# Attention followed by a feed-forward layer: two products split by head pair, two casts on ScalarE

## The chip, the cores and the metric

The kernel runs on one core of one Trainium2 chip. Five engines work side by side and meet at semaphores: TensorE (PE in the profile; its weight loads are shown as PEld), VectorE (DVE), ScalarE (ACT), GpSimd (POOL) and SyncE (SP), which here only issues DMAs. The metric is device time in microseconds; of several runs the median is taken. Lower is better.

## The reference

```python
# q, k, v: [8 batches, 8 heads, 576 positions, 64], float32
scores = (1 / 8) * q @ k^T                       # per batch and head
mask   = (i // 64) >= (j // 64)                  # causal in blocks of 64
attn   = softmax(where(mask, scores, -1e9))
x      = (attn @ v), heads side by side          # 4608 rows x 512
h      = x @ w_in                                # 512 -> 2048
g      = h * sigmoid(beta * h)
out    = g @ w_out                               # 2048 -> 512, float32
```

## The kernel before

**Attention.** Work is cut into 32 units `u = 4 * b + c`: a batch `b` and a pair of heads `c`. For the first two batches (`b < QB`) each unit's Q and K come by DMA into a float32 staging tile `ST` (L618, on SP's queue; six slots), are cast to bf16 into `QKn` (L625; POOL does most, DVE those named by `onp`), transposed on PE (L634) and copied from PSUM to `QKT` by DVE (L642). From batch 2 on the transposition is a DMA (L672). Scores are matmuls of `QKT` on 64-row tiles (L708, and L443 where a loaded weight is used again). ACT takes the exponential into `E` (L724, L736), DVE zeroes masked corners (L730, L732), PE multiplies with `V` (L764), DVE takes reciprocals of the sums (L776) and normalises into `xq` (L783; ACT does it for unit 1 in ten small copies, L788). For the first three batches PE transposes `xq` (L813) and DVE or, for units 2 and 3, ACT copies it to `xT` (L823, L821); later a DMA does it (L800). `xT` holds the feed-forward input with features on the partitions: slice `c` of it comes from head pair `c`.

**Feed-forward.** Nine chunks `r` of 512 rows. For each of 16 column blocks `j` of `w_in`, PE adds four 128-feature matmuls in one PSUM bank (L1000, function `fh`, one matmul for each head pair `c`), ACT takes a tanh (L1010), DVE forms `gT` (L1014). The second product is written plainly for chunk 0 (L1036) and as a seven-product scheme on half tiles for the others (L921).

**Order.** Nothing in the code fixes the engines' instruction order by hand. Every operation is entered with `P.op(engine, duration, function, deps, tiles, prio)`; `Plan.schedule` walks through a modelled time and gives each free engine the ready operation of lowest `prio` (on PE ties go to the earlier entered, elsewhere to the earlier ready). It hands out buffer slots and PSUM banks as it goes; an operation that gets a slot waits for the last users of it. So a small change of durations or priorities can reorder everything planned after it, and the waits with it. PE also gets filler matmuls (L523, L525) in modelled time before 50 us. `pr(u)` gives the attention priorities: 40 to 70 for batch 1; the feed-forward operations of chunk 0 have 1000 + `j`.

What the change touches: the cast of Q and K (`fn`, L625), the priority of the copy to `QKT` (`fc`, L642) and the creation of the first product (`fh`, L1000), whose dependencies `xd` name the `xT` copies of all four pairs of the batches in the chunk. Chunk 0 lies inside batch 0, so `xd` has four entries there.

Of the kernel before, what the change touches and what calls it, by code (L numbers as in the profile page):

```python
# [4 lines left out]
ACT = mybir.ActivationFunctionType  # L5
# [354 lines left out]
def bass_blockwise_causal_attn__then__act_swish_beta_kernel(  # L360
# [10 lines left out]
    with es:  # L371
        def sb(name, shape, dt):
# [5 lines left out]
        PARTS = [((0, 4, "SP", range(6)), (4, 8, "SP", range(2)), (4, 8, "POOL", range(2, 6)))] + [((0, 8, "SP", range(6)),)] * 7  # L378
        GROUPS = [((0,), (1,), (2,), (3,))] + [((0, 1), (2, 3))] * 7
        NS = 6  # L380
        JOIN = (2,3,4,5,6,7)
        NO = 4
        FAST = range(1, NRC)
# [4 lines left out]
        ST6 = [s[0:96].rearrange("p t d -> p (t d)")[:, 768 * i:768 * i + 768].rearrange("p (h j d) -> p h j d", h=2, j=6)  # L388
               for s in ST for i in range(3)]
# [4 lines left out]
        QKn = [sb(f"QKn{i}", [128, 2, 2, 768], bf16) for i in range(NQ)]  # L394
# [26 lines left out]
        P = Plan()  # L421
# [6 lines left out]
        def mm(n):  # L428
            return max(n / 2.4 + 3, 55.0)
# [4 lines left out]
        def dve_t(n):  # L434
            return (n + 125) / 0.96
# [34 lines left out]
        for i in range(NQ):  # L470
# [5 lines left out]
            o = P.op("POOL", 200, mk(lambda g, i=i: g.memset(Vn[i][:, 4, :, 64:66], 0.0)), prio=-5)  # L476
# [6 lines left out]
        for i in range(NQ, NE + 1):  # L483
# [8 lines left out]
                  deps=[bt, c2], tiles=[tb], lat=400, mode="full", prio=5)  # L492
# [5 lines left out]
        win, wout = [], []  # L498
# [18 lines left out]
        for i in range(NFILL):  # L517
# [10 lines left out]
            n = 125  # L528
            o = P.op("PE", n, ff, deps=[c2, c4], tiles=[tf], lat=n, mode="full", prio=1e6 + i)
# [6 lines left out]
        for b in range(B):  # L536
            ts, t = P.tile("Vs"), P.tile("V")
# [3 lines left out]
            for h0, h1, e, tt in PARTS[b]:  # L541

                vs = []
                for i in tt:
# [9 lines left out]
                    n = (h1 - h0) / 8 * (1 if i < 4 else 0.25)  # L554
                    if e == "SP":
                        o = P.op("SP", 300 + 550 * n, fv, tiles=[ts], xfer=1400 * n,
                                 prio=3.5 + 0.1 * (h0 > 0) if b == 0 else 4 * b + (3.5 if b < 2 else 0.5),
                                 dma=["d_V", h0, 1])
                    else:
                        o = P.op("POOL", 150 + 1450 * n, fv, tiles=[t], xfer=1400 * n, prio=-30 if b == 0 else 4 * b + (3.5 if b < 2 else 0.5), dma=["d_VP", h0, 1])  # L560
# [8 lines left out]
                n = 5 if 4 in tt else len(tt)  # L569
                for g0 in range(h0, h1, 2):  # L570
                    g1 = g0 + 2

                    def fw(g, e, ts=ts, t=t, g0=g0, g1=g1, n=n):
                        return g.tensor_copy(Vn[t.slot][:, 0:n, g0:g1, 0:64], Vs[ts.slot][:, 0:n, g0:g1, :])  # L574

                    o = P.op("POOL", 60 + 60 * n * (g1 - g0), fw, deps=[*vs, *ones, *vzero], tiles=[ts, t],
                             prio=4 * b + 0.5 - (38.5 - 4.6 * (h0 > 0)) * (b < 1))
# [23 lines left out]
        for u in range(NU):  # L601
            b, c = divmod(u, NPAIR)
            Tv = tl[b]
            p = c % 2
            if p == 0:

                tn, tt_ = P.tile("QKn"), P.tile("QKT")
                turned = []
                casts = []
            if b < QB:  # L610

                turned = []
                for w, (nm, src) in enumerate((("Q", q), ("K", k))):
                    ts, pt = P.tile("ST"), P.tile("P1")
                    early6.append(ts)

                    def fl(g, e, ts=ts, src=src, b=b, c=c):
                        return [g.dma_start(ST6[ts.slot].rearrange("p h j d -> p h (j d)"),  # L618
                                            src[b, 2 * c:2 * c + 2].rearrange("h (p j) d -> p h (j d)", j=6))]

                    o = ld[nm, u] = P.op("SP", 420, fl, tiles=[ts], xfer=1170, prio=u, dma=["d_S", 0, 1])
                    o.pkt = 80.0

                    def fn(g, e, ts=ts, tn=tn, p=p, w=w):
                        return g.tensor_copy(QKn[tn.slot][0:96, p, w, :].rearrange("p (j h d) -> p j h d", j=6, h=2),  # L625
                                             ST6[ts.slot].rearrange("p h j d -> p j h d"))

                    onp = u not in (0, 3) or w == 1
                    o = P.op("POOL" if onp else "DVE", 850 if onp else 750, fn, deps=[o], tiles=[ts, tn],
                             prio=-40 + 3 * u if onp else -1)  # L630

                    def ft(g, e, tn=tn, pt=pt, p=p, w=w):
                        for i in range(6):
                            z = g.transpose(PSb[:, pt.slot, 96 * i:96 * i + 96],  # L634
                                            QKn[tn.slot][0:96, p, w, 128 * i:128 * i + 128], identB[0:96, 0:96])
                        return z

                    o = P.op("PE", 6 * 43, ft, deps=[o, c4], tiles=[tn, pt, tt_], lat=6 * 43 + 170, mode="full",
                             prio=pr(u))

                    def fc(g, e, pt=pt, td=tt_, p=p, w=w):
                        return g.tensor_copy(QKT[td.slot][:, p, w, 0:576].rearrange("c (p j) -> c p j", j=6),  # L642
                                             PSb[:, pt.slot, 0:576].rearrange("c (j p) -> c p j", j=6))

                    o.rest = 400.0 if b else 0.0

                    turned.append(P.op("DVE", dve_t(576), fc, deps=[o], tiles=[pt, tt_], prio=-5 if b < 1 else .5))
            elif p == 0:

                for w, (nm, src) in enumerate((("Q", q), ("K", k))):  # L650
                    ts = P.tile("S4")

                    def fl(g, e, ts=ts, src=src, b=b, c=c):
                        return [g.dma_start(STh[ts.slot], src[b, 2 * c:2 * c + 4].rearrange("h t d -> (h t) d").rearrange(
                            "(i p) d -> p i d", p=128))]

                    o = P.op("SP", QKI, fl, deps=[o for t in early6 for o in t.users] if b == QB else [],
                             tiles=[ts], xfer=QKX, prio=u, dma=["d_S4", 0, 1])
                    for i in range(2):
                        ld[nm, u + i] = o  # L660
                    for a in range(2):
                        def fn(g, e, ts=ts, tn=tn, a=a, w=w):
                            x = STh[ts.slot][:, 9 * a:9 * a + 5, :]
                            x = bass.AP(x.tensor, x.offset, [x.ap[0], [64, 5], [256, 2], [1, 64]])
                            return g.tensor_copy(  # L665
                                QKn[tn.slot][:].rearrange("p a w n -> p (a w n)")[:, 640 * (2 * a + w):][:, 0:640]
                                .rearrange("p (t h d) -> p t h d", t=5, h=2), x)

                        casts.append(P.op(CAST, 740, fn, deps=[o], tiles=[ts, tn], prio=u))

                def ft(g, e, tn=tn, td=tt_):
                    return [g.dma_start_transpose(QKT[td.slot][:].rearrange("c a w (t n) -> c (a w t) n", n=128),  # L672
                                                  QKn[tn.slot][:].rearrange("p a w n -> p (a w n)")[:, 0:2560])]

                turned = [P.op("SP", 3250, ft, deps=casts, tiles=[tt_, tn], xfer=3200, prio=-1, dma=["d_T", 0, 1])]
# [3 lines left out]
            if b not in JOIN or p == 0:  # L679
# [4 lines left out]
                for grp in visits:  # L684
# [3 lines left out]
                    def fq(g, e, pst=pst, grp=grp, tqk=tqk, b=b):  # L688
                        keep = {}
                        for (uu, g0), ps in zip(grp, pst):  # L690
# [4 lines left out]
                            for t, q0, q1, off in blocks:  # L695
# [17 lines left out]
                    n = sum(220 if g0 < 3 else 60 for _, g0 in grp)  # L713
                    o = P.op("PE", n, fq, deps=cps, tiles=list({id(x): x for x in pst}.values()) + [tqk] + [tes[uu] for uu in sorted({uu for uu, _ in grp})] * (b > 0),
                             lat=n + 200, mode="row", prio=pr(u) + .2 if len(grp) == 4 else pr(u + 1) + .1 if grp[0][0] > u else
# [4 lines left out]
            for g0 in range(4):  # L720
                o, ps = qk[g0]
# [76 lines left out]
            if b >= XB:  # L798
# [5 lines left out]
                n = len(blocks(b))  # L804
# [184 lines left out]
        for r in range(NRC):  # L989
            row = RC * r  # L990
# [4 lines left out]
            for j in range(NJ):  # L995
                ph, tt = P.tile("P1"), P.tile("th")

                def fh(g, e, ph=ph, j=j, row=row):
                    for c in range(4):
                        z = g.matmul(PS[:, ph.slot, :], w_in[:, c, 128 * j:128 * j + 128], xT[:, c, row % RX:row % RX + RC],  # L1000
                                     start=(c == 0), stop=(c == 3))
                    return z

                o = P.op("PE", 4 * mm(512), fh, deps=xd + [win[j // 4]], tiles=[ph, tg], lat=4 * mm(512) + 170,
                         mode="full", prio=1000 + 100 * r + j)

                hs.append(o)

                def fs(g, e, ph=ph, tt=tt, j=j):
                    return g.activation(th[tt.slot][:], PS[:, ph.slot, :], ACT.Tanh, scale=beta[:, j:j + 1])  # L1010
                a = P.op("ACT", act_t(512, 1), fs, deps=[o, bC], tiles=[ph, tt], lat=act_t(512, 1) + 93, prio=0)

                def fg(g, e, ph=ph, tt=tt, tg=tg, j=j):
                    return g.scalar_tensor_tensor(out=gT[tg.slot][:, j, :], in0=th[tt.slot][:], scalar=1.0,  # L1014
                                                  in1=PS[:, ph.slot, :], op0=ALU.add, op1=ALU.mult)
                gs.append(P.op("DVE", dve_t(512), fg, deps=[a] + (spare.users + spare_x.users if r == 1 else []), tiles=[ph, tt, tg], prio=0))
# [113 lines left out]
```

## Time and profile before

| | us |
|---|---|
| median of 5 runs | 334.65 |
| lowest and highest | 334.15, 339.23 |
| the profiled execution, its own time | 335.34 |
| its span, first to last instruction | 333.5 |
| busy: PE | 322.7 (97%) |
| busy: DVE, ACT, POOL | 222.5, 213.0, 85.5 |
| mean granted clock of TensorE | 0.995 |

The span begins with the first instruction and is 1.84 us shorter than the execution's own time. Busy shares are means over stages with different limits; matmul durations are modelled at their ends, so a busy PE can still be slower than its best. In the rows for DMAs, SPq is SP's queue: the time beside a row is how long the issuing took, not how long the transfer did. The groups that the change touches, each with its count, busy time, mean in ns and idle time of the engine before it:

```profile
L1000 PE MATMUL PS<-xT,w_in 128*128 128x512 bf16 x542 | 130.7, 381 | 2.8 <-issue 0.5
```

### The profile page before, as it was taken

The page shows a single profiled execution, that of the slowest core. Times are in us where ns is not written, and L with a number is a line of the kernel's source. Part 1 is how long each engine was busy: PE and PEld are TensorE (multiplying, and loading weights), DVE is VectorE, ACT ScalarE, POOL GpSimd, SP SyncE. Part 2 cuts the span into 40 slices and gives each one's busy share as a digit, 9 for nine tenths or more (in the row PEclk, how much of TensorE's full clock was granted, in tenths as well). Part 3 has the DMA queues.
Part 4 walks back from the last instruction along what each step waited for, and adds up shares of the span by engine and source line. Part 5 has one row for each costly group of instructions (what it writes and reads, how often), then busy time and mean ns, then how long its engine had stood idle before and what let it go on. Part 6 is the DMA issues. An engine that isn't in the chain of part 4 may idle for free.

```text
span 333.5 us, 7478 instructions
## 1 busy us (share of the span) xinstructions
PE 322.7 (97%) x3112; PEld 204.5 (61%) x3090; DVE 222.5 (67%) x448; ACT 213.0 (64%) x324; POOL 85.5 (26%) x127
## 2 busy tenths in 40 slices
PE   7988999999999999999999999999999999999996
PEld 4565445544677457764676567566466766666685
DVE  4637866479783697457966595668567685666742
ACT  2865994189357886768758857884885645544521
POOL 7746182074082053103520630330000000000000
PEclk9997999999999999999999999999999999999999
DMA  7999999999999999999999998977102210110023
GB/s 199 225 234 234 200 217 210 195 279 221 204 268 216 159 206 195 211 206 198 194 191 198 203 269 185 192 134 132 34 31 41 85 51 33 44 52 31 0 97 126
DMA packets 154993, 53.41 MB, mean 160 GB/s; under 512 B 139072, under 2 KB 154448, under 8 KB 154960
## 3 DMA queue, kind: packets, MB, share of 16 engines
q1 hardware_dynamic: 141200, 40.19, 62.2%
q0 software_dynamic: 5568, 4.36, 8.3%
q10 hardware_dynamic: 8192, 8.39, 8.1%
q8 instruction: 24, 0.39, 0.5%
q14 instruction: 9, 0.07, 0.1%
HBM read 36.71 MB, written 9.44 MB: 138 GB/s over the span
## 4 chain that ended last, share of the span: by engine, by line
PE 83%; DVE 4%; ACT 4%; DMA 2%; issue 2%; SPq 2%; POOL 1%; ACTq 0%; POOLq 0%
PE PS L1000 34%; PE PS L921 28%; PE PS L764 7%; PE PS L708 7%; PE PS L1036 4%; DMA Vs<-in_v_dram 2%; DVE gT L1014 2%; SPq L548 2%; ACT E L724 1%; PE PS L813 1%; ACT th L1010 1%; DVE OV L885 1%; PE PS L634 1%; ACT xq L788 1%; DVE xq L783 0%
## 5 line engine op out<-in xcount | busy, mean ns | idle before, releaser
L1010 ACT ACTIVATE th<-PS,beta 128x512 f32<-128x512 f32 x144 | 96.4, 699 | 60.8 <-PE PS L1000 59.8
L1000 PE MATMUL PS<-xT,w_in 128*128 128x512 bf16 x542 | 130.7, 381 | 2.8 <-issue 0.5
L1014 DVE SCALAR_TENSOR_TENSOR gT<-th,PS 128x512 f16<-128x512 f32 x144 | 95.1, 681 | 32.7 <-ACT th L1010 31.9
L724 ACT ACTIVATE E<-PS 128x1024 bf16<-128x1024 f32 x93 | 92.0, 1028 | 28.5 <-PE PS L708 28.5
L1000 PEld LDWEIGHTS PS<-xT,w_in 128*128 128x128 bf16 x576 | 53.6, 98 | 55.8 <-issue 2.1
L921 PE MATMUL PS<-w_out,gT 128*128 128x256 f16 x512 | 63.0, 273 | 0.0
L921 PEld LDWEIGHTS PS<-w_out,gT 128*128 128x128 f16 x512 | 49.0, 98 | 12.1 <-issue 1.3
L574 POOL CAST Vn<-Vs 128x640 bf16<-128x640 f32 (+1 forms) x28 | 21.3, 761 | 95.5 <-DMA Vs<-in_v_dram 94.1
L665 POOL CAST QKn<-ST 128x640 bf16<-128x640 f32 x48 | 37.8, 788 | 27.0 <-DMA ST<-in_k_dram 13.7
L708 PE MATMUL PS<-QKT 64*128 64x320 bf16 (+4 forms) x328 | 36.9, 299 | 0.2 <-ACT E L724 0.2
L764 PEld LDWEIGHTS PS<-Vn,E 128*128 128x128 bf16 x930 | 30.9, 97 | 4.7 <-POOL Vn L574 1.0
L942 ACT ACTIVATE ost<-PS 128x512 f32<-128x512 f32 x32 | 19.4, 606 | 21.5 <-PE PS L921 21.5
L764 PE MATMUL PS<-Vn,E 128*128 128x65 bf16 x930 | 31.8, 193 | 0.8 <-POOL Vn L574 0.8
L921 PE MATMUL PS<-OV 128*128 128x256 f16 x256 | 32.0, 273 | 0.0
L708 PEld LDWEIGHTS PS<-QKT 64*128 64x128 bf16 (+1 forms) x328 | 13.5, 96 | 26.2 <-issue 11.7
L921 PEld LDWEIGHTS PS<-OV 128*128 128x128 f16 x256 | 24.2, 98 | 5.8 <-issue 1.1
L885 DVE TENSOR_TENSOR OV<-gT 128x1024 f16<-128x1024 f16 x32 | 24.5, 775 | 1.1 <-PE PS L921 0.6
L783 DVE TENSOR_TENSOR xq<-PS,inv 128x640 bf16<-128x640 f32 x30 | 24.6, 821 | 0.7
L730 DVE MEMSET E<- 64x64 uint32 x62 | 6.9, 112 | 24.0 <-ACT E L724 21.9
L945 DVE SCALAR_TENSOR_TENSOR ost<-PS,ost 128x512 f32<-128x512 f32 x22 | 15.1, 688 | 8.0 <-PE PS L921 5.5
L921 PE MATMUL PS<-OV,gT 128*128 128x256 f16 x128 | 16.1, 273 | 0.0
L1036 PE MATMUL PS<-w_out,gT 128*128 128x512 f16 x64 | 15.5, 380 | 0.0
(65 smaller groups left out, 176.9 us busy)
## 6 DMA issues: line engine op xcount, KB each, us to landing
out_dram<-ost ACTq DMA_DIRECT2D x32, 256.0 KB, 3.7
ST<-in_q_dram SPq DMA_DIRECT2D x12, 576.0 KB, 5.5
ST<-in_k_dram SPq DMA_DIRECT2D x12, 576.0 KB, 7.9
Vs<-in_v_dram SPq DMA_DIRECT2D x24, 256.0 KB, 3.9
ST<-in_q_dram SPq DMA_DIRECT2D x8, 288.0 KB, 6.3
ST<-in_k_dram SPq DMA_DIRECT2D x8, 288.0 KB, 6.7
w_in<-in_moe_w_in_dram POOLq DMA_DIRECT2D x4, 512.0 KB, 10.3
w_out<-in_moe_w_out_dram POOLq DMA_DIRECT2D x4, 512.0 KB, 10.1
```

The source lines that it names most:

```text
L574: return g.tensor_copy(Vn[t.slot][:, 0:n, g0:g1, 0:64], Vs[ts.slot][:, 0:n, g0:g1, :])
L665: return g.tensor_copy(QKn[tn.slot][:].rearrange("p a w n -> p (a w n)")[:, 640 * (2 * a + w):][:, 0:640] .rearrange("p (t h d) -> p t h d ...
L708: z = g.matmul(o, QKT[tqk.slot][r, uu % 2, 1, 128 * t + y:128 * t + m + y], x)
L724: return g.activation(E3[es_(te)][:, g0, :, :], PS[:, ps.slot:ps.slot + 2, :], ACT.Exp, scale=0.125)
L764: z = g.matmul(o, eblk(te, t, i, h), Vn[Tv.slot][:, t, 2 * c + h, 0:65], start=(t == 0), stop=(t == i))
L783: return g.tensor_tensor(xq[xq_(tx)][:].rearrange("p i (h d) -> p h i d", h=2), both(pv, 0, 64), x, ALU.mult)
L885: return P.op("DVE", dve_t(SZ * HC / 2), mk(lambda g: g.tensor_tensor(fo(), fx(), fy(), op)), deps=deps, tiles=tiles, prio=prio)
L921: x = g.matmul(PS[:, pw.slot, HM * w:HM * w + HM], fa()[:, j, 128 * w:128 * w + 128], fb()[:, j, :], start=first and (pair or w == 0) and ...
L1000: z = g.matmul(PS[:, ph.slot, :], w_in[:, c, 128 * j:128 * j + 128], xT[:, c, row % RX:row % RX + RC], start=(c == 0), stop=(c == 3))
L1010: return g.activation(th[tt.slot][:], PS[:, ph.slot, :], ACT.Tanh, scale=beta[:, j:j + 1])
L1014: return g.scalar_tensor_tensor(out=gT[tg.slot][:, j, :], in0=th[tt.slot][:], scalar=1.0, in1=PS[:, ph.slot, :], op0=ALU.add, op1=ALU.mult)
L1036: z = g.matmul(PS[:, po.slot, 0:d1 - d0], gT[tg.slot][:, j, 128 * w:128 * w + 128], w_out[:, j, d0:d1], start=(j == 0), stop=(j == NJ - 1))
```

## The change

Three things. `CASTA` gives the casts of unit 4 (the first pair of the second batch), Q and K, to ACT with priority -1; they were POOL's, with a priority of -28. `SPLIT` makes the first two products (`j` 0 and 1) of chunk 0 four operations each, one matmul per head pair; each waits for the `xT` copy of its own pair, for the weights, and for the part before it. Only the last part is a complete sum. And the copy of unit 4's transposed Q and K on DVE gets priority 0 in place of 0.5.

```diff
+        SPLIT = {(0, j): [(0,), (1,), (2,), (3,)] for j in range(2)}
+        CASTA = {(4, 0), (4, 1)}
...
-                        return g.tensor_copy(QKn[tn.slot][0:96, p, w, :].rearrange("p (j h d) -> p j h d", j=6, h=2),
-                                             ST6[ts.slot].rearrange("p h j d -> p j h d"))
+                        x = QKn[tn.slot][0:96, p, w, :].rearrange("p (j h d) -> p j h d", j=6, h=2)
+                        y = ST6[ts.slot].rearrange("p h j d -> p j h d")
+                        return g.activation(x, y, ACT.Copy) if e == "ACT" else g.tensor_copy(x, y)
...
-                    o = P.op("POOL" if onp else "DVE", 850 if onp else 750, fn, deps=[o], tiles=[ts, tn],
-                             prio=-40 + 3 * u if onp else -1)
+                    o = P.op("ACT" if (u, w) in CASTA else "POOL" if onp else "DVE", 850 if onp else 750, fn, deps=[o], tiles=[ts, tn],
+                             prio=-1 if (u, w) in CASTA else -40 + 3 * u if onp else -1)
...
-                    turned.append(P.op("DVE", dve_t(576), fc, deps=[o], tiles=[pt, tt_], prio=-5 if b < 1 else .5))
+                    turned.append(P.op("DVE", dve_t(576), fc, deps=[o], tiles=[pt, tt_], prio=-5 if b < 1 else 0 if u == 4 else .5))
...
-                def fh(g, e, ph=ph, j=j, row=row):
-                    for c in range(4):
+                def fh(g, e, ph=ph, j=j, row=row, cs=range(4)):
+                    for c in cs:
...
-                o = P.op("PE", 4 * mm(512), fh, deps=xd + [win[j // 4]], tiles=[ph, tg], lat=4 * mm(512) + 170,
-                         mode="full", prio=1000 + 100 * r + j)
-
-                hs.append(o)
+                o = None
+                for cs in SPLIT.get((r, j), [range(4)]):
+                    n = len(cs) * mm(512)
+                    o = P.op("PE", n, lambda g, e, fh=fh, cs=cs: fh(g, e, cs=cs),
+                             deps=[x for i, x in enumerate(xd) if i % 4 in cs] + [win[j // 4]] + ([o] if o else []),
+                             tiles=[ph, tg], lat=n + 170, mode="full", prio=1000 + 100 * r + j)
+                    hs.append(o)
```

## The prediction

> **What bounds the kernel now.** I read the page first, then the stretches around the change, then the timelines of ScalarE (ACT), SP and POOL there.
>
> ```profile
> PE   7988999999999999999999999999999999999996
> ACT  2865994189357886768758857884885645544521
> PEclk9997999999999999999999999999999999999999
> PE 83%; DVE 4%; ACT 4%; DMA 2%; issue 2%; SPq 2%; POOL 1%; ACTq 0%; POOLq 0%
> ```
>
> TensorE (PE) is busy in nearly every slice after the start, and the chain that ended last is 83% PE. Time can be won where PE has no ready work, and the first row names only the first four slices (33 us) and the very end. In the fourth slice the granted clock drops too. The stretches, each with busy time of PE, weight loads, VectorE (DVE), ACT and POOL, clock, DMA share and GB/s:
>
> ```profile
> 26.30:29.70 3.40, 2.26 (x30) 1.71 (x32) 2.76 (x6) 1.58 (x5) 3.09 (x5) 0.99 1.24 207
> 29.70:33.10 3.40, 3.40 (x22) 1.50 (x19) 1.86 (x3) 1.78 (x3) 1.21 (x2) 0.51 1.18 263
> 32.00:44.00 12.00, 11.90 (x91) 5.48 (x89) 9.49 (x20) 11.73 (x18) 2.76 (x4) 0.96 1.03 215
> 60.00:316.80 256.80, 254.38 (x2356) 160.41 (x2335) 179.89 (x347) 170.98 (x255) 53.97 (x68) 1.00 0.75 150
> ```
>
> PE is only 66% busy from 26.3 to 29.7; then it runs 3.4 us at half clock; from 32 to 44 ACT is busy 11.73 of 12 us. From 60 to 316.8 PE loses 2.4 of 256.8 us. So there are two regimes: to about 43 us the pace is set by when ACT gets its first product and its first scores, after that by PE alone. This is ACT before the saturated part (start, duration, and in brackets its idle time and what ended it):
>
> ```profile
> 26.46 0.71 ACT L821 ACTIVATE xT<-PS 128x512 bf16<-128x512 bf16 x2
> 28.58 0.71 ACT L821 ACTIVATE xT<-PS 128x512 bf16<-128x512 bf16 x2 [1.41 <-PE PS L813]
> 31.03 0.69 ACT L1010 ACTIVATE th<-PS,beta 128x512 f32<-128x512 f32 x1 [1.74 <-PE PS L1000]
> 32.00 1.94 ACT L724 ACTIVATE E<-PS 128x1024 bf16<-128x1024 f32 x2 [0.28 <-PE PS L708]
> ```
>
> The last xT copy (pair 3) ends at 29.29; only then may the first feed-forward product start, although pair 0's xT was copied by 26.1. PE does the product's four matmuls from 29.57 to 30.99, half of it at low clock, and the batch-1 scores stand behind them. ACT gets its first input at 31.03. The loads and casts behind the scores:
>
> ```profile
> 17.45 0.99 SPq L618 DMA_DIRECT2D ST<-in_q_dram  x1
> 18.48 0.46 SPq L618 DMA_DIRECT2D ST<-in_k_dram  x1
> 26.50 0.31 SPq L618 DMA_DIRECT2D ST<-in_q_dram  x1
> 25.61 5.43 POOL L625 CAST QKn<-ST 96x768 bf16<-96x768 f32 x6
> 33.16 0.82 POOL L625 CAST QKn<-ST 96x768 bf16<-96x768 f32 x1 [2.12 <-DMA ST<-in_q_dram]
> 24.30 0.72 ACT L788 ACTIVATE xq<-PS,inv 128x64 bf16<-128x64 f32 x3 [2.60 <-DVE inv L776]
> ```
>
> Each of the first two loads (Q and K of pair 4) has 5.6 us to landing, so 23.05 and 24.1. POOL, issuing weight DMAs, casts them only from 25.61. ACT idles 2.60 us before 24.30.
>
> [...]
>
> **The change, part by part.** I take instruction order from the built programs, durations from before.
>
> *Two casts move from POOL to ACT.* ACT has no such cast in the trace. Its 512-column copy takes 606 ns (L942) and 1024 columns take 1028 (L724): 0.824 ns a column, so 768 columns cost 606 + 256 x 0.824 = 817 ns by estimate. Bounds: DVE's 584 ns for the same cast (L625)[...]. The Q cast stands before the ten xq copies of pair 1: 23.1 to 23.9, inside the 2.60 us idle, before 24.30. The K cast follows these copies: 26.46 to 27.28. Behind it stand both xT copies; pair 2's slips from 26.46 to about 27.7, also because PE now transposes pair 1 ahead of pair 2, and it hides because pair 3 ends later still. POOL loses 2 x 0.82 us, so pair 5 is cast from 25.61 instead of 27.3 and pair 6 is done by about 29.1.
>
> *Queues.* Pair 7's Q load waits for a staging slot that ACT's cast now frees, near 24.0 instead of 26.50; pair 7's K and batch 1's V follow from 26.5, against 27.39 and 27.74. No load is added or crosses another. From 25.5 to 28.5 the DMAs move 206 GB/s, from 30 to 33 268: the ring was short of work there. Filling 3 us at the higher rate moves 0.19 MB[...]: loads up to the w_out weights come 0 to 1 us earlier.
>
> *The two products in parts.* The same eight matmuls (warm 215 to 229 ns each, from four in 0.86 and twelve in 2.76 us), as eight operations with a wait each; only the last part of a product releases the tanh. One filler matmul (about 0.1 us) goes. The order from 25.8: Q transposes of pair 4 (0.43), transposes of pairs 1 and 2 (26.61 to 27.6; the first waits for xq at 26.46 as before), the first part (0.22), Q/K transposes of pairs 4 and 5, pair 3's transposes, the second part, pair 5's K, then the pair-4 scores, then the last two parts.
>
> *DVE.* The QKT copies of pair 4 get a better priority: one (0.76) goes ahead of pair 3's norm (0.82), which now ends near 27.95 instead of 27.11. Then pair 1's xT (0.51), to 28.45, and pair 4's K copy, to 29.2. Pair 3's transposes end near 29.3, its xT copy near 30.05 instead of 29.29: **the last part of the product gets later by 0.75 us, the scores earlier.** Pair 5's K transposes (0.3) wait for a bank until 29.2, then the scores take 0.6 (warm, 37.46 to 38.06 in the trace): done at 30.4. If the clock drops again, 30.75.
>
> *ACT's start.* Before: tanh at 31.03, then a gap of 0.28, so its gapless stretch counts from 31.31. After, the two exps start at 30.45, with the tanh behind them (the product is complete by 30.9, the exps last to 32.4). The same fifteen ACT instructions follow up to 42.2. Gain 31.31 - 30.45 = 0.86 with full clock, 0.5 with half. Bounds: 0.1 if casts and bank waits take their worst values, 1.2 if PE finds no bank wait. PE's long run of 28 product matmuls, 42.94 before, starts about 0.8 earlier.
>
> *After 43 us.* PE has the same matmuls but for the filler and the same 99 changes between row-packed and full tiles. The long order is planned anew from there; to this I give no mean value and +-1 us. Sum against the profiled execution: 335.34 (span 333.5 and 1.84 around it) - 0.8 = 334.5. It lies 0.69 above the median of the runs shown, 334.65, so on that scale **333.8**.
>
> **The rivals.** *R1, w_out takes the gain (0.06).* The second products need the w_out quarters, issued at 46.66 and later at about 9 us to landing. If the V load that gates them does not come earlier, PE reaches the second quarter 0.8 us before it lands. For it: PE loses 0.38 of 17.1 us from 42.9 to 60. Against: the fuller ring. Time 334.6.
>
> *R2, slower: a transpose queue in the wrong order (0.22).* In the new SP order batch 4's first two QKT transposes stand behind an xT transpose which before stood between them. Before, QKT issued at 132.62 and the xq for that xT was ready at 136.27 (DVE, L783). In the new order SP may stand up to 3.65 us on it. That QKT, 8.4 us from issue to landing (132.62 to 141.05), was first read at 145.41: 4.35 us of slack. It decides only if it grows past that: with about 3 us more, from a later norm, PE and ACT lack scores and lose what filler products do not cover, an estimate of 2 to 2.5 us after subtracting the gain. Time 334.65 - 0.8 + 2.2 = 336.0. Against: feed-forward products fill PE, 254 of 257 us.
>
> *R3, a bigger win (0.17).* The half-clock window goes (it cost 3.4 x 0.49 = 1.7 us of PE work, of which ACT's saturation hides most), the ring gives a full 1 us, and the new order loses less between 90 and 260 us. Then 0.8 + 0.7 + 0.7 = 2.2: 332.4.
>
> *That the change does nothing* is excluded: the orders differ from PE's ninetieth instruction on.
>
> **How the numbers follow.** The forecast case, an earlier start carried to the end, gets 0.55 and has its own range 332.9 to 334.5. A measurement here can tell 0.3%, 1.0 us, from no change, so the forecast stands near that bound: half of its chance (0.275) is faster, half the same. Faster: 0.275 + 0.17 = 0.45. Same: 0.275 + 0.06 = 0.33. Slower: R2, 0.22. The range 331.9 to 335.9 leaves out about a tenth on each side.
>
> **What would show it.** Right: two casts on ACT near 23.1 and 26.5 of about 0.8 us; the second batch's exps before the first tanh and near 30.4; ACT gapless from there; the 28-matmul run near 42.1; pair 7's Q load issued near 24. Undecided until seen: the clock from 29.7 to 33. Wrong: xq of pair 1 later than 24.3 (the Q load landed late), the exps not before 31, a wait for w_out near 55, or SP standing on an xT transpose while QKT is wanted.

## The result, and the profile after

The changed kernel takes 336.21 us (median of 44 runs, 334.04 to 339.67) where the kernel before takes 334.76 (79 runs): a ratio of 1.0051, 95% interval 1.0035 to 1.0066. It is slower by about 1.7 us, and outside the predicted range. (The ratio and the 1.7 leave out the slow runs, 12 of the 79 and 3 of the 44, each more than 1.5% above the fastest of its kernel; the two medians of all runs differ by 1.45.) The profiled execution took 337.52 us, with a span of 335.6 (before: 335.34 and 333.5).

The first page of the changed kernel, the same rows as before:

```profile
PE   6897999999999999999998999999999999999996
ACT  2785994188656894687647867884894645545521
PEclk9997999999999999999999999999999999999999
PE 59%; SPq 22%; DMA 10%; DVE 2%; issue 2%; POOL 2%; ACT 1%; POOLq 0%; ACTq 0%
```

PE still fills its slices, with an 8 in the twenty-second (176 to 185 us). The chain that ended last is no longer 83% PE: it now runs through SP's queue and transfers. That row is a pointer and no measure; in a second profile of the same kernel it reads 87% PE again. The stretches that the prediction used (busy time of PE, weight loads, DVE, ACT, POOL, then clock, DMA share and GB/s):

```profile
26.30:29.70 3.40, 1.61 (x24) 1.22 (x23) 1.64 (x5) 1.14 (x3) 1.40 (x2) 0.98 1.18 247
29.70:33.10 3.40, 3.40 (x23) 1.52 (x19) 1.97 (x3) 1.49 (x3) 1.36 (x3) 0.52 1.19 229
32.00:44.00 12.00, 11.57 (x87) 4.91 (x84) 8.41 (x19) 11.66 (x19) 1.70 (x3) 0.96 0.98 189
60.00:316.80 256.80, 252.51 (x2344) 159.17 (x2325) 176.34 (x346) 170.15 (x254) 53.77 (x68) 1.00 0.78 151
```

The half-clock window is there as before (0.52 of full speed over these 3.4 us, 0.51 before). In the long stretch PE is busy 252.51 us instead of 254.38. Records are missing from both traces, so this difference is an indication only; further down PE's progress is read from its weight loads, whose records are complete in all traces. ACT at the start, and SP's load of pair 7's Q:

```profile
22.07 0.83 ACT L629 ACTIVATE QKn<-ST 96x768 bf16<-96x768 f32 x1
25.85 0.88 ACT L629 ACTIVATE QKn<-ST 96x768 bf16<-96x768 f32 x1
30.33 0.71 ACT L824 ACTIVATE xT<-PS 128x512 bf16<-128x512 bf16 x2 [2.51 <-PE PS L816]
32.33 1.94 ACT L727 ACTIVATE E<-PS 128x1024 bf16<-128x1024 f32 x2 [1.28 <-PE PS L711]
...
22.92 0.31 SPq L620 DMA_DIRECT2D ST<-in_q_dram  x1
```

The casts take 0.83 and 0.88 us, near where they were expected; pair 7's Q load goes out 3.6 us earlier; the exps come ahead of the first tanh. But in this profile they start at 32.33, later than the 32.00 of before, which was one of the prediction's signs of being wrong ("the exps not before 31"). The first place of loss farther on is the first product of chunk 2, near 109 us. PE, DVE and the weight loads there:

```profile
105.08 1.08 PE L767 MATMUL PS<-Vn,E 128*128 128x65 bf16 x30
106.62 0.82 DVE L786 TENSOR_TENSOR xq<-PS,inv 128x640 bf16<-128x640 f32 x1
107.18 1.01 PE L711 MATMUL PS<-QKT 64*128 64x320 bf16 x12 [0.15 <-ACT E L727]
108.12 0.53 PE L816 MATMUL PS<-identB,xq 128*128 128x128 bf16 x5
108.69 0.52 DVE L826 COPY xT<-PS 128x512 bf16<-128x512 bf16 x2 [0.34 <-PE PS L816]
109.26 0.55 PEld L1003 LDWEIGHTS PS<-xT,w_in 128*128 128x128 bf16 x4 [0.72 <-DVE xT L826]
```

Nothing stands on PE between the transposes (L816) of the batch's last pair and the product that reads them, so PE sits through DVE's copy. The kernel before has 8 matmuls of a second product there:

```profile
105.47 0.52 PE L813 MATMUL PS<-identB,xq 128*128 128x128 bf16 x5
105.79 1.03 PE L708 MATMUL PS<-QKT 64*128 64x320 bf16 x12
106.75 1.05 PE L921 MATMUL PS<-OV,gT 128*128 128x256 f16 x8
107.85 1.67 PE L1000 MATMUL PS<-xT,w_in 128*128 128x512 bf16 x7
```

The second place is the first product of chunk 4. The row of the page for the first products, SP's queue, the last pair's norm on DVE, two pieces of the chain, and PE, all of the changed kernel:

```profile
L1003 PE MATMUL PS<-xT,w_in 128*128 128x512 bf16 x541 | 130.0, 380 | 4.3 <-DMA xT<-xq 1.0
...
165.07 3.25 SPq L803 DMA_TRANSPOSE xT<-xq  x2
168.37 3.13 SPq L675 DMA_TRANSPOSE QKT<-QKn  x1
171.55 2.55 SPq L803 DMA_TRANSPOSE xT<-xq  x2
...
163.83 0.82 DVE L786 TENSOR_TENSOR xq<-PS,inv 128x640 bf16<-128x640 f32 x1
...
172.84 4.00 DMA xT<-xq
176.83 0.27 issue
177.10 1.67 PE PS L1003 x7
...
177.10 1.24 PE L1003 MATMUL PS<-xT,w_in 128*128 128x512 bf16 x5 [1.03 <-DMA xT<-xq]
```

SP's row at 171.55 (two transposes) is the last pair of batch 4; DVE had finished its `xq` at 164.65 (163.83 + 0.82), so it stood 6.9 us behind another pair's transposes and a `QKT` transpose. PE idled 1.03 us for it. Before, SP issued it ahead of that `QKT` transpose:

```profile
165.39 3.08 SPq L800 DMA_TRANSPOSE xT<-xq  x2
168.52 3.19 SPq L672 DMA_TRANSPOSE QKT<-QKn  x1
...
171.96 1.07 PE L764 MATMUL PS<-Vn,E 128*128 128x65 bf16 x30
173.08 1.67 PE L1000 MATMUL PS<-xT,w_in 128*128 128x512 bf16 x7
```

and chunk 4 began without a wait (173.08, behind V products that ended at 173.03). PE came to it earlier, too.

### The profile page after: what moved, and what is told of

Read it like the earlier page. It is cut to its first block, busy times and chain, and to the rows that moved or that the text cites. A ratio compares the mean times of both kernels' runs of the same rounds, so it can differ in the third digit from the quotient of the medians.

```text
span 335.6 us, 7477 instructions
## 1 busy us (share of the span) xinstructions
PE 322.2 (96%) x3110; PEld 204.6 (61%) x3089; DVE 220.0 (66%) x448; ACT 214.2 (64%) x326; POOL 83.5 (25%) x125
## 4 chain that ended last, share of the span: by engine, by line
PE 59%; SPq 22%; DMA 10%; DVE 2%; issue 2%; POOL 2%; ACT 1%; POOLq 0%; ACTq 0%
PE PS L1003 26%; PE PS L924 23%; SPq L550 11%; SPq L657 5%; PE PS L711 5%; PE PS L767 5%; DMA ST<-in_k_dram 4%; SPq L675 4%; DMA QKT<-QKn 3%; SPq L553 2%; DMA ST<-in_q_dram 2%; DMA xT<-xq 1%; DVE gT L1020 1%; ACT th L1016 1%; ACT E L727 1%
## 5 line engine op out<-in xcount | busy, mean ns | idle before, releaser
L1003 PE MATMUL PS<-xT,w_in 128*128 128x512 bf16 x541 | 130.0, 380 | 4.3 <-DMA xT<-xq 1.0
L1003 PEld LDWEIGHTS PS<-xT,w_in 128*128 128x128 bf16 x576 | 53.4, 98 | 58.2 <-DVE gT L1020 2.0
L924 PE MATMUL PS<-w_out,gT 128*128 128x256 f16 x512 | 62.6, 273 | 0.0
L924 PEld LDWEIGHTS PS<-w_out,gT 128*128 128x128 f16 x512 | 48.9, 98 | 11.3 <-issue 1.1
L924 PE MATMUL PS<-OV 128*128 128x256 f16 x256 | 31.8, 273 | 0.2 <-DVE OV L888 0.2
L924 PEld LDWEIGHTS PS<-OV 128*128 128x128 f16 x256 | 24.2, 98 | 6.1 <-issue 0.8
L888 DVE TENSOR_TENSOR OV<-gT 128x1024 f16<-128x1024 f16 x32 | 23.6, 748 | 1.0 <-PE PS L924 0.6
L645 DVE COPY QKT<-PS 128x576 bf16<-128x576 bf16 x16 | 12.0, 757 | 7.7 <-PE PS L637 7.4
L735 DVE MEMSET E<- 64x128 uint32 x31 | 5.1, 165 | 17.8 <-ACT E L727 16.9
```

The costliest lines, as they stand in the source:

```text
L888: return P.op("DVE", dve_t(SZ * HC / 2), mk(lambda g: g.tensor_tensor(fo(), fx(), fy(), op)), deps=deps, tiles=tiles, prio=prio)
L924: x = g.matmul(PS[:, pw.slot, HM * w:HM * w + HM], fa()[:, j, 128 * w:128 * w + 128], fb()[:, j, :], start=first and (pair or w == 0) and ...
```

## The experiments

**Reading.** One execution differs from the next by more than the change is worth: a half-clock window near 30 us is there in some (0.51 and 0.52 over 3.4 us in the first profiles of the two kernels) and not in others (the profiled execution of before_again has a mean clock of 1.000). So three things are compared. First, the ratio of times. Second, the gaps of PE. Third, PE's progress by its weight loads in the first products (L1003 or L1000): from the 41st of them (at 42 to 46 us) to the first of chunk 5 (near 203 us) all kernels here have done the same matmuls, and after it they need the same 129.0 to 129.2 us to the end, so this *stretch* compares orders. The gaps and the stretch are worked out from the starts in the trace. Where a kernel's order is forced, a table gives each engine its operations one by one and the planner may take only the next; lines in such kernels are shifted by 71 from the kernel that they were made from (L1074 for L1003, L995 for L924, L874 for L803):

```diff
+                    if len(order[e]) == len(ORDER[e]):
+                        continue
+                    want = ORDER[e][len(order[e])]
...
+                        if want != (-1 if o.fill else o.idx):
+                            continue
```

**Both kernels once more, and their halves exchanged.** The order up to about 43 us (head) and the order after it (tail) can be exchanged, since both kernels have done the same operations by then.

```diff
 x1_newhead_oldtail
-ORDER = head and tail of the changed kernel
+ORDER = head of the changed kernel, tail of the kernel before
 x2_oldhead_newtail
-ORDER = head and tail of the kernel before
+ORDER = head of the kernel before, tail of the changed kernel
```

Both kernels again, unchanged:

> The kernel before unaltered, for a second profile: ratio 1.000 within 0.15%. If the pause near 27.5 us is steady here it is again 0.4 to 0.8 us; if it varies by as much as between the two first profiles, the head cannot be read from one profile.

> The changed kernel unaltered, for a second profile. If the long pause of TensorE near 27.3 us belongs to the change it is over 1.3 us again and the 28-matmul run starts later than 43.3; if it was chance it is near 0.5 and that run starts before 42.9. Time 336.2 either way within 0.3%.

The exchanges:

> New head (split products, both casts on ScalarE, their order up to about 43 us), then the order of before for everything later. Theory H (the start is later: TensorE's pause inside the pair-4/5 transposes grew from 0.5 to 1.6-1.8 us and the rest follows): about 0.5% slower than before, 336.4. Theory T (the order planned anew after 43 us loses it): the head's own 0.6 us at most, ratio 1.000 to 1.002, 334.8 to 335.4.

> The head of before (no split, casts on GpSimd), then the order of the changed kernel for everything later. Theory H: like before, ratio 0.999 to 1.001. Theory T: 0.35 to 0.5% slower, 336.0 to 336.5, with TensorE gaps of about 1 us again where products wait for xT, near 108 and 175 us.

| | ratio to before, 95% interval | 41st load at, us | stretch, us |
|---|---|---|---|
| before (first profile) | | 44.46 | 159.99 |
| before_again | 1.0003 [0.9983, 1.0024] | 42.91 | 159.81 |
| x1_newhead_oldtail | 1.0003 [0.9977, 1.0029] | 42.54 | 159.78 |
| after (first profile) | 1.0051 [1.0035, 1.0066] | 45.05 | 161.41 |
| after_again | 1.0040 [1.0020, 1.0061] | 43.12 | 161.10 |
| x2_oldhead_newtail | 1.0071 [1.0044, 1.0099] | 43.01 | 162.29 |

The loss is in the tail, whichever head stands before it: 1.3 to 2.5 us on the stretch. The head gains little. The windows 100 to 112 and 165 to 180 us, before_again, then x1_newhead_oldtail, then after_again (in these three traces PE's records are complete):

```profile
100.00:112.00 12.00, 11.82 (x139) 7.30 (x133) 6.30 (x16) 8.89 (x15) 2.43 (x4) 1.00 1.14 208
165.00:180.00 15.00, 15.00 (x163) 9.94 (x158) 9.62 (x22) 11.00 (x17) 2.40 (x3) 1.00 1.02 190
```

```profile
100.00:112.00 12.00, 11.87 (x136) 7.42 (x133) 6.65 (x17) 8.88 (x15) 2.88 (x4) 1.00 1.12 214
165.00:180.00 15.00, 15.00 (x163) 9.82 (x157) 9.79 (x22) 10.59 (x16) 1.85 (x3) 1.00 1.02 185
```

```profile
100.00:112.00 12.00, 11.23 (x133) 7.20 (x129) 6.12 (x18) 8.64 (x13) 3.17 (x5) 1.00 1.23 218
165.00:180.00 15.00, 14.21 (x170) 10.58 (x165) 7.61 (x18) 9.66 (x14) 1.78 (x2) 1.00 0.78 158
```

PE loses 0.77 and 0.79 us in these two windows with the new tail, 0.1 to 0.2 and nothing with the old one. Over the stretch, 1590 matmuls in both, the time between starts beyond each kind's usual distance is 1.3 us more with the new tail (after_again) than with the old (x1). Of this, about 0.8 is transposes to first product (near 107) and 0.86 scores to first product (near 174); all other pairs together are 0.4 better in the new order, mostly because a wait near 53 us is gone. x2's larger loss is the wait near 174 at 1.38 in place of 0.86, that wait near 53, and one of 0.26 near chunk 5.

**Which of the two edits makes the new tail.** Planned anew with one edit alone:

```diff
 split_only
-        CASTA = {(4, 0), (4, 1)}
+        CASTA = set()
-... prio=-5 if b < 1 else 0 if u == 4 else .5
+... prio=-5 if b < 1 else .5
 casts_only
-        SPLIT = {(0, j): [(0,), (1,), (2,), (3,)] for j in range(2)}
+        SPLIT = {}
```

> Only the two products in four parts; casts on GpSimd and the old copy priority; everything planned anew, and the plan gives SP exactly the order of the changed kernel. If the loss comes with the order planned after the split, 1.004 to 1.007 slower; if it came from the casts, 1.000.

> Only the two casts on ScalarE and the copy priority, planned anew; the plan keeps SP's order of before and differs from it on TensorE around the start alone. If the loss comes with the order planned after the split, 0.998 to 1.002; if the casts themselves cost (ScalarE queue, earlier loads against the w_in loads), 1.004 or more.

split_only: 1.0054 [1.0034, 1.0074], with gaps of 0.92 us at 107.1 and 1.05 at 174.5, stretch 161.44. casts_only: 0.9993 [0.9968, 1.0019], neither gap, stretch 159.73. Its SP order is that of the kernel before, that of split_only is the changed kernel's. So the split, not the casts, sets off the other order.

**SP's whole queue exchanged.** Each kernel with all of SP's order from the other:

```diff
 x3_after_old_sp
-ORDER["SP"] of the changed kernel
+ORDER["SP"] of the kernel before
 x4_before_new_sp
-ORDER["SP"] of the kernel before
+ORDER["SP"] of the changed kernel
```

> The changed kernel on all engines but SP, whose DMAs are issued in the order of before (QKT transpose ahead of the V loads that overtook it). Theory S (SP's order makes the second batch pair's QKT late and this empties TensorE near 107 and 174 us): ratio to before 1.000 to 1.002, both gaps under 0.3 us. Theory C (the compute engines' new order is itself short of filler there): still 1.004 or more, the gap near 107 us stays about 0.8.

> The kernel before on all engines but SP, whose DMAs are issued in the order of the changed kernel. Theory S: 1.003 to 1.006 slower, QKT of the second pair of batch 2 lands 3 to 4 us later. Theory C: 0.999 to 1.002, because the lateness is covered by the old compute order.

1.0221 [1.0176, 1.0266] and 1.0190 [1.0146, 1.0233]: both far slower, each with one large gap of PE, 4.4 us at 139.7 and 5.4 us at 171.8. SP's order fits only the compute order that it was planned with, so this tells the two causes apart badly. One thing it does tell: in x3 the gap near 107 stayed (1.04 us), so that one does not come from SP's order.

**One exchange at a time.** f1 moves pair 11's transposes on PE, f2 the last pair of batch 4 on SP, f12 does both, b2 does the reverse of f2 to the kernel before:

```diff
 f1_tr_first, PE near 105 us
+L887 transposes of pair 11
 L782 scores x12
-L887 transposes of pair 11
 L1074 first product of chunk 2
 f2_xt_first, SP near 168 us (b2_xt_last: the reverse, in the kernel before)
+L874 xT<-xq x2, last pair of batch 4
 L746 QKT<-QKn
-L874 xT<-xq x2, last pair of batch 4
```

> The changed kernel with its own order on every engine, but on PE the transposes of pair 11 (the last of batch 2) stand ahead of the twelve score matmuls before them, so that the way from the normed xq to the first product of chunk 2 has these matmuls as cover. Theory G (the loss is two waits of PE for the last pair of a batch, near 107 and near 174 us): the gap near 107 falls from 0.8 to 1.0 us to under 0.4, the gap near 174 stays; 0.5 us of 1.7 comes back, ratio to before about 1.003. Rival D (the loss lies spread over the whole new order, the two gaps are only the visible part and PE catches up behind them): ratio stays at 1.004 to 1.006. A third outcome: the transposes now wait for xq themselves, the gap moves in front of them at its old size, and the ratio stays.

> The changed kernel with its own order on every engine, but on SP the two xT transposes of the last pair of batch 4 are issued ahead of the QKT transpose that stood before them. Theory G: the first product of chunk 4 no longer waits, the gap of 0.9 to 1.4 us near 174 goes, 0.9 us comes back, ratio to before about 1.002. Rival D: ratio stays at 1.004 to 1.006. Rival Q: the QKT transpose becomes late by what xT gained (SP now stands on xq with QKT behind it), a gap of 1 us or more appears at the next batch's scores, and the ratio stays or grows.

> Both edits together. Theory G: both gaps gone, PE otherwise full, so the two gains add: ratio to before 1.000 to 1.001. Rival D: 1.004 to 1.006. If the gaps are only half of it: 1.002 to 1.003.

> The kernel before with its own order on every engine, but on SP the two xT transposes of the last pair of batch 4 are issued behind the QKT transpose that stood after them, as the changed kernel does it. Theory G: a gap of about 1 us appears on PE near 173, in front of the first product of chunk 4, and the kernel is 0.2 to 0.3% slower than before. Rival: the order before has other products to put in PE there (its way from the last reciprocal to chunk 4 is 12.0 us, the new order's 15.2), the xT comes later and nobody waits: ratio 1.000, no gap.

f1: 1.0056 [1.0032, 1.0079], the third outcome. The gap moved: PE now waits for `xq` ahead of the transposes, and for the mask behind the first product (first and fourth line). The gap near 174, which was to stay, grew (last line), and the clock was lower behind it (0.62 from 176.2 to 179.6, 0.88 from 179.6 to 183.0); so this profile's stretch, 164.40, does not tell what the first gap is worth:

```profile
105.56 0.53 PE L887 MATMUL PS<-identB,xq 128*128 128x128 bf16 x5 [0.48 <-DVE xq L857]
105.90 1.03 PE L782 MATMUL PS<-QKT 64*128 64x320 bf16 x12
106.89 1.04 PE L1074 MATMUL PS<-xT,w_in 128*128 128x512 bf16 x4
108.30 1.08 PE L838 MATMUL PS<-Vn,E 128*128 128x65 bf16 x30 [0.37 <-DVE E L806]
...
176.21 2.01 PE L1074 MATMUL PS<-xT,w_in 128*128 128x512 bf16 x6 [1.97 <-DMA xT<-xq]
```

f2: 1.0036 [1.0015, 1.0056]; f12: 1.0023 [0.9999, 1.0046]. In both the gap near 174 is gone, but PE comes earlier to chunk 5, and in f2 it waits there for the same kind of transfer. SP's queue and PE's row in f2:

```profile
195.39 5.65 SPq L746 DMA_TRANSPOSE QKT<-QKn  x1
201.09 1.28 SPq L874 DMA_TRANSPOSE xT<-xq  x1
...
203.81 1.90 PE L1074 MATMUL PS<-xT,w_in 128*128 128x512 bf16 x8 [0.40 <-DMA xT<-xq]
```

Again an xT behind a `QKT` transpose; its `xq` was ready at 195.51. f2's stretch is still 161.25 (f12: 160.99); where its gain went is told below. b2 is the strongest of the four: 1.0166 [1.0128, 1.0204], far more than either theory gave it. PE waits in front of chunk 4, and its clock falls behind the wait (second line: 0.54 of full speed over 3.3 us):

```profile
173.00:176.70 3.70, 1.07 (x32) 0.94 (x29) 1.04 (x2) 0.14 (x1) 0.00 (x0) 0.95 0.81 195
176.70:180.00 3.30, 3.26 (x8) 1.04 (x8) 0.62 (x1) 0.69 (x1) 0.00 (x0) 0.54 0.97 195
```

This one exchange on SP takes 2.67 us of waiting, and some 1.5 us more (3.3 x 0.46, an estimate) through the clock; the stretch is 164.08, 4.3 longer than in before_again.

**The way to chunk 2 begun earlier, and the next xT too.** g1 begins pair 11's scores and V product earlier by one group of eight matmuls each; f3 adds f2's exchange. f4 is f2 with the same exchange at batch 5, f5 is f3 with it. after_third is the changed kernel on the chip of f4 and f5.

```diff
 g1_chain_full, PE near 97 us (first exponential of pair 11 ahead of an eviction on ACT)
 L995 x8
+L782 scores of pair 11
 L995 x8
 L887 transposes of pair 10
-L782 scores of pair 11
 L995 x16
+L782 scores of pair 12
+L838 V product of pair 11
 L995 x8
-L782 scores of pair 12
-L838 V product of pair 11
 L995 x8
+L887 transposes of pair 11
 L782 scores x12
-L887 transposes of pair 11
 L1074 first product of chunk 2
 f4_two_xt_first, SP near 195 us, beside f2's exchange
+L874 xT<-xq, last pair of batch 5
 L746 QKT<-QKn
-L874 xT<-xq, last pair of batch 5
```

> The changed kernel with its own order, but near 97 to 107 us the way to the first product of chunk 2 is begun earlier, as the kernel before does it: on PE the score matmuls of pair 11 and its product with V stand one group of eight second-product matmuls earlier each, its transposes ahead of the next scores, and ACT takes the first of its exponentials ahead of an eviction. PE's work between is the same. Theory G: the gap near 106 goes (under 0.3 us), 0.6 to 0.8 us comes back at full clock, but part of it is given back at the gap near 174, which PE now reaches earlier (1.4 to 2 us there, as in the first attempt); ratio to before 1.003 to 1.005. Rival D (the loss is spread over the order): 1.004 to 1.006 with the gap near 174 at 0.9 to 1.1 us as before.

> The same, and on SP the last pair of batch 4 transposed ahead of the QKT transpose before it. Theory G: both gaps gone; at full clock 333.8 to 334.3 us against 335.0 to 335.8 of the changed kernel and 333.6 to 334.0 of the kernel before, ratio to before 1.000 to 1.001. If the gaps are only part of it, as the edit of SP's queue alone left it (335.0 at full clock): 1.002 to 1.003, and the time must be lost in many small waits.

> As f2_xt_first (SP transposes the last pair of batch 4 ahead of the QKT transpose before it), and the same once more one batch later: the xT transpose of batch 5's last pair ahead of the QKT transpose before it. In f2_xt_first PE reached chunk 5 earlier and waited there 0.4 us for this xT, so part of what the first exchange won was given back. Theory G2 (the waits for the last pair's xT on SP are one chain, and closing the next one keeps the gain): from the 41st weight load of the first products to the first of chunk 5 the profile has 160.6 to 160.9 us (161.25 in f2_xt_first, 161.1 to 161.4 in the changed kernel, 159.8 before), ratio to before 1.001 to 1.003. Rival D (the loss only changes its place): 161.1 or more and 1.003 to 1.005.

> As f3_both_gaps with the second exchange of f4_two_xt_first. If the queue order on SP and the short way near 107 us are the loss: 160.5 to 160.9 us on the same stretch, ratio 1.000 to 1.002. Rival D: 161.1 or more, and 1.002 or more.

> The changed kernel itself once more, on the same chip as the other two: 1.004 to 1.005 and 161.1 to 161.4 us on the stretch.

| | ratio to before, 95% interval | stretch, us |
|---|---|---|
| g1_chain_full | 1.0028 [1.0002, 1.0053] | 161.28 |
| f3_both_gaps | 1.0007 [0.9979, 1.0035] | 161.17 |
| f4_two_xt_first | 1.0029 [1.0008, 1.0050] | 160.17 |
| f5_all_three | 1.0013 [0.9993, 1.0033] | 160.98 |
| after_third | 1.0039 [1.0016, 1.0063] | 161.07 |

Where the stretch changes is seen from its pieces. Each entry is the difference to after_third in us, from the weight loads:

| | to chunk 2 | chunk 2 to 3 | chunk 3 to 4 | chunk 4 to 5 | sum |
|---|---|---|---|---|---|
| f2 (xT at chunk 4) | 0.00 | +0.27 | -0.73 | +0.63 | +0.18 |
| f4 (xT at chunks 4 and 5) | +0.01 | -0.04 | -0.73 | -0.14 | -0.90 |
| f12 (f1 and f2) | -0.09 | +0.50 | -0.73 | +0.24 | -0.08 |
| g1 (way to chunk 2) | +0.02 | +0.65 | -0.73 | +0.28 | +0.21 |
| f3 (g1 and f2) | 0.00 | +0.58 | -0.73 | +0.25 | +0.10 |
| f5 (g1 and f4) | 0.00 | +0.76 | -0.73 | -0.12 | -0.09 |

f4 is what the theory asked: no wait for an xT at chunk 4 or 5, 0.9 us off the stretch, and 0.36 left of the loss against before_again. SP in f4 near 195 us, and PE's start of chunk 5:

```profile
197.14 2.74 SPq L874 DMA_TRANSPOSE xT<-xq  x1
199.93 3.81 SPq L746 DMA_TRANSPOSE QKT<-QKn  x1
...
204.94 1.67 PE L1074 MATMUL PS<-xT,w_in 128*128 128x512 bf16 x7
```

f2 wins the same 0.73 at chunk 4 and gives back 0.63 on the way to chunk 5; another 0.27 is lost ahead of the exchange, in one wait near 127 us. At chunk 2 nothing was won: from pair 10's V product to the first product of chunk 2 the changed kernel needs 11.27 us, and g1, f3 and f5 need 11.27 too, with waits of 0.33 (for an eviction) and 0.25 in other places. Behind that product they lose about 0.5, where a V product now waits for its mask, as in f1. This is most of what f5 lacks against f4.

g1 holds a surprise: SP's order is untouched, and yet the gap near 174, which was expected to grow, is gone. SP issued the last pair of batch 4 at 167.54, in after_third at 169.29:

```profile
167.54 2.55 SPq L874 DMA_TRANSPOSE xT<-xq  x2
...
173.93 1.67 PE L1074 MATMUL PS<-xT,w_in 128*128 128x512 bf16 x7 [0.16 <-issue]
```

So the order on SP makes the wait possible, and how far SP lags sets its size: with this same order PE idled 0.79 to 1.03 us in three profiles of the changed kernel, 1.97 in f1, and here not at all for an xT. Why SP was ahead in g1 was not tested.

The times are too coarse for such differences. f4's ratio, 1.0029, has an interval that overlaps after_third's, and f5's is better than f4's. But fewer of f5's runs had a lower granted clock (5 of 22 against 8), and f4's median is the lower one both for these runs and for the others. The runs with a mean clock of at least 0.998, all on this chip, have medians of 334.28 (f4), 334.45 (f5), 334.71 (after_third) and 333.50 (the kernel before): the order of the stretches, but the steps lie within the scatter. No version beats the kernel before.

## Why the prediction was wrong

**The step that failed** is "After 43 us": "The long order is planned anew from there; to this I give no mean value and +-1 us." On the stretch behind 43 us the runs showed a loss of 1.3 to 1.6 us in three profiles of the changed kernel, and of 2.5 in the one with the old head. Nor was there as much to win as to lose: the 2.4 us that PE seemed to lose from 60 to 316.8 us were mostly missing records. In before_again, whose records are complete, PE is busy 256.62 of these 256.80 us. By this measure a new order could hardly be better there, only worse. The order treated as neutral has two places where the last pair of a batch reaches its chunk late. One, on SP, is shown by the profiles: an xT transpose behind a `QKT` transpose, 0.9 us of the stretch together with the next one (f4 undoes both, b2 makes the first in the kernel before, where the time shows it as well). This is one profile for each, and f4's time agrees without being able to measure it. The other, near 107 us, is seen in every profile that keeps the new tail's order there and in none with the old; moving operations only moved the wait, so its share, some 0.4 us by what f4 leaves, is not shown by a run.

**The mis-sized term** is the head: "Gain 31.31 - 30.45 = 0.86 with full clock". Without a half-clock window near 30 us, the 41st load comes at 42.91 and 43.01 with the old head (before_again, x2), and at 42.04 to 43.12, median 42.69, in seven profiles with the new one: 0.3 us, less than these seven differ among themselves. The base was a disturbed one. The profile used for 31.31 had the window; in before_again, which does not, the first tanh starts at 30.17 and the exps at 30.76, while the new head's exps start at 29.87 (x1) and 30.46 (after_again). The sum is then -0.3 + 1.3 to 1.6 = +1.0 to +1.3 us, against a measured 1.3 to 1.7.

**Right:** the casts (0.83 and 0.88 us for an estimated 0.82), their places on ACT, pair 7's Q load (22.92, expected near 24), exps ahead of the first tanh, the same matmuls in the stretch. The earlier loads brought nothing that could be told apart: the last of the first six loads of batch 1's V was issued at 39.48 before and landed at 42.60; after, at 40.47 and 42.84. Nor do the rows show that the ring was short of work from 25.5 to 28.5, where 206 GB/s were moved: the DMA share was 1.21 there, and 1.18 from 30 to 33, with 268 GB/s.

**The rivals.** R1 was not seen: from 43 to 60 us PE is busy 16.99 of 17.00 us in f2, which has the changed kernel's order there. R3 neither: the new order loses more, not less. Its remark that most of a half-clock window's 1.7 us is hidden does not hold: on each of the five chips the kernel before's runs below a mean clock of 0.998 have a median 1.5 to 1.8 us above that of the others. R2 named the right queue and nearly the right sum (336.0), but the other way round and elsewhere: it feared `QKT` behind an xT near 130 us; it was xT behind `QKT` near 170. That the sum came near was chance. The new order of SP was known, so the place could have been found by holding each xT against the first product that reads it; how long the wait would be could not, as g1 shows.

**The clock is not the cause.** 16 of 44 runs of the changed kernel had a mean granted clock under 0.998, and 102 of 242 of the kernel before. On the chip of after_third, the runs above it have medians of 334.71 (14 runs) and 333.50 (30), so the loss is there at full clock.

## What to carry to other kernels

When a planner makes the order, an edit in the first tenth is also a new draw for the rest, and where one engine is busy 256.6 of 256.8 us that draw has nearly nothing to win. It deserves a number of its own, on the side of loss: list, for each batch, the last operand of the next stage and what its queue has ahead of it. Judge a start-up gain from several profiles, because one can hold a half-clock window (0.51 over 3.4 us in the first profile of the kernel before) that the next has not (before_again). A gap that is closed is worth what the next waits leave of it (in f2, none of 0.73 us), so measure progress to a later landmark, in pieces, and not the gap.

## What the runs showed of the hardware

**PE paused near 27 us.** Counting all of PE's recorded instructions (matmuls, weight loads and waits), PE stops behind its 705th in before, 0.75 us in L813 (from 27.39 to 28.14, start to start), and behind its 704th in after, 1.83 us in L637 (from 27.28 to 29.11). The length differs from profile to profile: 0.3 to 2.4 us in the others, and no pause in before_again. In before the pause ends 2.54 us after a packet of 16384 bytes of the instruction queue begins (at 25.60), in after 2.58 us (at 26.53). The DMA share is 1.20 from 25.6 to 28.2 in before and 1.18 from 26.5 to 29.2 in after. The page's row for that queue (packets, MB, share) and the changed kernel's row behind the pause, which names no releaser:

```profile
q8 instruction: 24, 0.39, 0.5%
...
29.11 0.60 PE L637 MATMUL PS<-identB,QKn 96*128 96x96 bf16 x10 [1.63 <-issue]
```

The packet and the pause lie close in time; what PE waited for was not shown.

**Two stalls of 2 us or more were followed by half clock.** In f1 a wait of 1.97 us near 174 us was followed by 3.4 us at half clock from 177.0 (0.62 from 176.2 to 179.6, 0.88 from 179.6 to 183.0), in b2 one of 2.67 us likewise from 176.3 (0.95 from 173.0 to 176.7, 0.54 from 176.7 to 180.0). After gaps of 0.8 to 1.4 us the clock stayed full: after a gap of 1.03 us in after it is 1.00 from 177.1 to 184.0, with gaps of 0.79 (after_again) and 1.38 (x2) it is 1.00 from 165 to 180. In the 3.4 us ahead of the low clock PE was still busy for 1.44 us (f1) and 1.18 us (b2). Where the line between these cases lies was not tested. By these clocks 3.4 x 0.38 + 3.4 x 0.12 = 1.7 us of PE's work is lost in f1 and 3.7 x 0.05 + 3.3 x 0.46 = 1.7 us in b2, an estimate; with it such a wait cost 1.9 and 1.6 times its length.
